# First product of the first four groups made token slot by token slot, and three smaller moves in a fused attention and feed-forward kernel

## The chip, the cores and the metric

The kernel runs on one core of one Trainium2 chip. The metric is the device time of one execution in microseconds (us), and the median of several executions is quoted. The kernel before took 298.68 us when it was first measured (three runs, 298.0 to 299.06). With each experiment it was run again on the same chip, and an experiment is compared with those runs only. All outputs of all kernels told here were correct.

An execution counts as slow when it lies more than 1.5% above the fastest of the same kernel.

## The reference

There are two parts in a row. Linear attention over 8 batches of 8 heads, 576 tokens, 64 features:

```python
q_p = phi(q, cos_w, sin_w); k_p = phi(k, cos_w, sin_w)   # relu, then cos and sin weights: 128 features
kv  = einsum('bhsf,bhsd->bhfd', k_p, v);  z = sum(k_p, axis=2)
num = einsum('bhsf,bhfd->bhsd', q_p, kv)
den = einsum('bhsf,bhf->bhs', q_p, z)[..., None] + 1e-06
x   = (num / den) with heads side by side: 4608 tokens x 512
```

and then a feed-forward layer on these 4608 tokens:

```python
h = x @ w_in                                 # 512 -> 2048
g = h * (1 / (1 + exp(-1.702 * h)))
out = g @ w_out                              # 2048 -> 512
```

## The kernel before

The tokens go in nine blocks of 512. In each block TensorE (PE) makes 16 groups of the first product (L278, "group 0" to "group 15", each of 128 hidden features), then the second product. Between these, pieces of the attention of the next batch are slipped in by a schedule `at(step, ...)`: q' and k' on DVE, the transposes of q' by DMA from the SP queue (`turn_q`), kv and z (`unit_kv`), and numerators (`unit_num`, 128 tokens, a "slot", at a time). The first batch has nothing to hide behind: its attention is the prologue.

```python
# order of the loads of the prologue, all from GpSimd's queue
load_main(0, "k", 0, 4)
load_main(0, "v", 0, 4)
load_main(0, "k", 4, 8)
load_main(0, "v", 4, 6)
load_main(0, "v", 6, 8)
...
# prologue, first product: three groups, 512 tokens wide, by quarters of the contraction as x comes
first = [mm_tile() for _ in range(3)]
for fc in range(3):
    mm1_first(fc, (0, 1), 0, TB)
    if fc == 1:
        turn_x0(0, 0, 4, 2, 3)
for fc in range(3):
    mm1_first(fc, (2,), 0, TB)
turn_x0(1, 0, 4, 3, 4)
for fc in range(3):
    mm1_first(fc, (3,), 0, TB, last=True)
    gelu(first[fc], fc)
...
def turn_q_at(b, c):                       # batch 1: q' turned by PE, copied out of PSUM by DVE
    t = at_tile()[:, 0].bitcast(BF16)...
    for h in range(H):
        nc.tensor.transpose(t[:, h], qn_slot(b, c)[:, h, :], ident[...])
    nc.vector.tensor_copy(q_slot(b, c)[:, :, 0:rows(c)], t)
...
# block i prepares batch b = i + 1
at(10, unit_num, 1, 4)                     # i == 1: the last 64 tokens of batch 1
at(22 + c // 2, turn_q_at, b, c)           # i == 0
at(k0 + c, turn_q, b, c)                   # i > 0: transposes by DMA
at(k1 - 1, prep_v, b, c)                   # v copied chunk by chunk
at(1, load_all, b + 1)                     # i > 0: the loads of the batch after
```

PSUM has two kinds of tile: four `mm` of one bank, two `at` of two banks. Matmuls on zeros (`warmup`) keep PE busy in the prologue.

## Time and profile before

| what | value | view |
|---|---|---|
| median of four runs of the first two rounds | 298.48 us | times |
| span of the profiled run | 296.7 us | page |
| PE busy | 97% of the span | page |
| first product at full size without a hole (group 4) | 23.43 us (the prediction and the expectations write 23.44) | PE timeline: 22.57 + 4 x 0.216 |
| group 4 to the first product after kv of batch 1 | 22.90 us | PE timeline: 46.33 - 23.43 |
| start of block 1 to slot 3's numerator of batch 2 | 24.48 us | PE timeline: 79.42 - 54.94 |

The lines of the profile that carry the argument are in the prediction below. Two of the page give the granted clock of TensorE, in tenths of full speed for each of 40 slices of the span (9 is 90% or more):

```profile
span 296.7 us, 5049 instructions
PEclk9999999999999999999999999999999999999999
```

(The clock record of this trace has it rise at 6.26 us and fall once, at 296.40. In it warm-up matmuls of 512 columns follow each other at 0.427 us before the rise and at 0.216 after it.)

### The profile page before, as it was taken

The numbers are of one execution on the slowest core, as the hardware profiler recorded it, in microseconds if no ns is written. First come the engines' busy times: TensorE is split into PE (matmuls) and PEld (weight loads), VectorE is DVE, ScalarE is ACT, GpSimd is POOL, SyncE is SP. The second block draws the span as 40 slices with busy tenths as digits, with TensorE's granted clock in tenths as the row PEclk, the third lists the DMA queues.
The fourth block names the chain that finished last, engine by engine and source line by source line (L and its number), as shares of the span: only waits on it lengthen the run. The fifth ranks groups of instructions, "written<-read, shape, count | busy, mean of one in ns | idle before, by whom it ended". The sixth has DMA issues, their size and how long they took to land.

```text
span 296.7 us, 5049 instructions
## 1 busy us (share of the span) xinstructions
PE 286.7 (97%) x1943; PEld 144.2 (49%) x1943; DVE 109.2 (37%) x363; ACT 121.4 (41%) x210; POOL 93.9 (32%) x117
## 2 busy tenths in 40 slices
PE   8779999999999999999999999999999999999994
PEld 3554456545444554455445544554455444444443
DVE  5850585772490158015811482148214200000000
ACT  5757401663126412651165116511651166127411
POOL 8443220620268025801690159004401200120021
PEclk9999999999999999999999999999999999999999
DMA  7999999699979967999799779975903610011033
GB/s 183 190 204 200 203 198 191 177 132 158 218 143 179 182 112 117 205 163 131 138 181 177 117 142 181 181 120 127 185 0 60 125 39 3 35 71 35 2 70 71
DMA packets 87303, 39.65 MB, mean 134 GB/s; under 512 B 57136, under 2 KB 85040, under 8 KB 87280
## 3 DMA queue, kind: packets, MB, share of 16 engines
q0 software_dynamic: 40848, 27.01, 59.7%
q1 hardware_dynamic: 46272, 12.20, 24.7%
q8 instruction: 15, 0.25, 0.3%
q10 hardware_dynamic: 160, 0.13, 0.2%
q14 instruction: 8, 0.07, 0.1%
HBM read 36.70 MB, written 9.44 MB: 155 GB/s over the span
## 4 chain that ended last, share of the span: by engine, by line
PE 89%; DMA 4%; ACT 3%; DVE 2%; issue 0%; DVEq 0%
PE mm L278 40%; PE mm L318 37%; DMA qT<-qn 4%; PE at L241 3%; PE at L262 3%; PE at L75 2%; PE mm L342 1%; ACT qT L362 1%; ACT kp L205 1%; DVE xb L270 1%; PE mm L409 1%; PE mm L371 1%; ACT xT L405 1%; PE at L222 0%; DVE qT L223 0%
## 5 line engine op out<-in xcount | busy, mean ns | idle before, releaser
L318 PE MATMUL mm<-w_out_sb,g 128*128 128x512 bf16 x560 | 128.7, 379 | 0.0
L278 PE MATMUL mm<-xT,w_in_sb 128*128 128x512 bf16 (+1 forms) x568 | 124.5, 378 | 0.0
L330 POOL DMA_DIRECT2D out_dram<-ysb x54 | 50.6, 941 | 174.3 <-ACT ysb L328 172.9
L283 ACT ACTIVATE g<-mm 128x512 bf16<-128x512 f32 x144 | 85.6, 597 | 47.3 <-PE mm L278 46.7
L278 PEld LDWEIGHTS <-w_in_sb 128*128 128x128 bf16 x568 | 54.7, 98 | 64.6
L318 PEld LDWEIGHTS <-g 128*128 128x128 bf16 x560 | 52.1, 97 | 57.0
L328 ACT COPY ysb<-mm 128x512 f32<-128x512 f32 x34 | 19.9, 585 | 98.2 <-PE mm L318 98.2
L245 DVE CAST kvs<-at 128x260 bf16<-128x260 f32 x14 | 5.4, 426 | 54.2 <-PE at L241 54.2
L270 DVE TENSOR_TENSOR xb<-at,inv 128x512 bf16<-128x512 f32 (+1 forms) x36 | 24.8, 690 | 1.2
L268 DVE TENSOR_SCALAR den<-at 128x8 f32<-128x8 f32 (+1 forms) x36 | 5.9, 164 | 46.5 <-PE at L262 46.5
L347 DVE COPY ysb<-mm 128x256 f32<-128x256 f32 x1 | 0.4, 426 | 59.4 <-PE mm L342 59.4
L207 DVE TENSOR_SCALAR qn<-q,cosw 128x512 bf16<-128x512 bf16 (+1 forms) x36 | 12.7, 357 | 13.6 <-DMA q<-in_q_dram 13.6
L262 PEld LDWEIGHTS <-qT 128*128 128x128 bf16 x272 | 12.9, 98 | 8.8 <-DMA qT<-qn 0.8
L262 PE MATMUL at<-kvs,qT 128*128 128x65 bf16 x272 | 14.3, 194 | 0.6 <-DMA qT<-qn 0.3
L207 DVE TENSOR_SCALAR qn<-q,sinw 128x512 bf16<-128x512 bf16 (+1 forms) x34 | 13.0, 381 | 0.0
L241 PEld LDWEIGHTS <-kp 128*128 128x128 bf16 (+1 forms) x288 | 10.1, 97 | 3.5 <-DVE vt L210 0.8
L241 PE MATMUL at<-vt,kp 128*128 128x65 bf16 (+1 forms) x288 | 11.3, 193 | 0.6 <-DVE vt L210 0.5
L86 POOL DMA_DIRECT2D v<-in_v_dram x10 | 8.5, 851 | 4.9 <-DMA v<-in_v_dram 2.5
L86 POOL DMA_DIRECT2D k<-in_k_dram x9 | 7.8, 864 | 2.7 <-DMA q<-in_q_dram 1.9
L230 ACT COPY xT<-at 128x512 bf16<-128x512 bf16 x4 | 2.4, 590 | 15.0 <-PE at L228 15.0
L75 PE MATMUL at<-warm 128*128 128x512 bf16 x19 | 7.2, 536 | 1.2 <-DVE eps L151 1.2
L207 DVE TENSOR_SCALAR kp<-k,cosw 128x512 bf16<-128x512 bf16 x24 | 8.4, 350 | 0.0
(75 smaller groups left out, 135.2 us busy)
## 6 DMA issues: line engine op xcount, KB each, us to landing
out_dram<-ysb POOLq DMA_DIRECT2D x38, 128.0 KB, 2.9
out_dram<-ysb POOLq DMA_DIRECT2D x16, 256.0 KB, 2.8
q<-in_q_dram POOLq DMA_DIRECT2D x7, 512.0 KB, 9.2
k<-in_k_dram POOLq DMA_DIRECT2D x6, 512.0 KB, 11.2
v<-in_v_dram POOLq DMA_DIRECT2D x6, 512.0 KB, 12.8
w_out_sb<-in_moe_w_out_dram POOLq DMA_DIRECT2D x4, 512.0 KB, 18.4
w_in_sb<-in_moe_w_in_dram POOLq DMA_DIRECT2D x3, 512.0 KB, 11.7
q<-in_q_dram SPq DMA_DIRECT2D x2, 512.0 KB, 4.6
```

What stands on the lines that cost most here:

```text
L75: nc.tensor.matmul(wps[:, 0], warm[:, 0:128], warm, start=True, stop=True)
L86: on.dma_start(out=state[b][n][:np_, t * D * h0:t * D * h1].rearrange("p (h e) -> p h e", h=h1 - h0), in_=SRC[n][b, h0:h1, 0:np_ * t, :].r ...
L207: nc.vector.tensor_scalar(oc, i, 0.0, wc, op0=MAX, op1=MUL)
L241: nc.tensor.matmul(kv[:, ds(h % 4 * (D + 1), D + 1)], kp[:r, c, h, :], vt[:r, c, h, 0:D + 1], start=(c == 0), stop=(c == last))
L262: nc.tensor.matmul(nm[:, h // 4, ds(h % 4 * (D + 1), D + 1)], q_slot(b, c)[:, h, :], state[b]["kvs"][:, h // 4, h % 4, 0:D + 1], start=Tru ...
L268: nc.vector.tensor_scalar(den[:r], nm4[:, :, :, D], 1e-6, None, op0=ADD)
L270: nc.vector.tensor_tensor(state[b]["xb"][:r, c].rearrange("p (n h) d -> p n h d", n=2), nm4[:, :, :, 0:D], inv[:r].unsqueeze(3).to_broadca ...
L278: nc.tensor.matmul(hps[:, c0:c1], w_in_sb[:, kc, ds(fc * 128, 128)], xT[:, kc, ds(i * TB + c0, c1 - c0)], start=(kc == 0), stop=(kc == KC ...
L283: nc.scalar.activation(g, hps, AF.Gelu_apprx_sigmoid)
L318: nc.tensor.matmul(yps, gT[fc][:, ds(t * 128, 128)], w_out_sb[:, fc, :], start=(fc == 0), stop=(fc == FC - 1))
L328: nc.scalar.copy(ysb, cur[t])
L330: nc.gpsimd.dma_start(out=out[row:row + (n - 1) * step + 1:step, :], in_=ysb[p0:p0 + n, :])
```

## The change

The change has three parts. In part A the prologue makes four groups of the first product instead of three, slot by slot as x comes (128, 128 and 256 tokens), turns x in the unused half of the bank that held the numerators, and loads k's upper half ahead of v's lower one. (It also has ACT copy all four pieces of the turned q', of which DVE copied one before, and loads the third group of w_in ahead of q's tail.) In part B the turned q' of batch 1 is copied out of PSUM by ACT instead of DVE, and its v by one DVE copy instead of six. In part C the numerator of batch 1's tail moves from step 10 to step 14 of block 1.

```diff
 # part A
+    load_main(0, "k", 4, 8)
     load_main(0, "v", 0, 4)
-    load_main(0, "k", 4, 8)
 ...
-    warmup(13)
+    warmup(12)
 ...
-    kv0(0, 4)
 ... (k' upper, numerators, turns and three groups of 512 columns)
+    kv_lo, kv_hi = mm_tile(), mm_tile()
+    kv0(kv_lo, 0, 4)
+    kv0(kv_hi, 4, 6)
+    na0 = num0(0, 0)
+    kv0(kv_hi, 6, 8)
+    product0(na0, den0(na0), 0, 0)
+    nb0 = num0(1, 0)
+    turn_x0(na0, 0, 0)
+    product0(nb0, den0(nb0, VE, (0, 1)), 1, 0, (0, 1))
+    product0(nb0, den0(nb0, VE, (1, 2)), 1, 0, (1, 2))
+    turn_x0(nb0, 1, 0, (0, 1))
+    first = [mm_tile() for _ in range(4)]
 ...
+    for fc in (0, 1):
+        mm1_first(fc, K4, 0, 128)
+    turn_x0(nb0, 1, 0, (1, 2))
 ... (128 to 256, then 256 to 512 in two halves of the contraction)
 # part B
-        nc.vector.tensor_copy(q_slot(b, c)[:, :, 0:rows(c)], t)
+        copy(q_slot(b, c)[:, :, 0:rows(c)], t)            # called with AC.copy
+    def prep_v_wide(b):
+        nc.vector.tensor_copy(vt[:96, :, :, 0:D], state[b]["v"][:96, 0:48 * D].rearrange(...))
 # part C
-                at(10, unit_num, 1, 4)
-                at(10, turn_x, 1, 4)
+                at(14, unit_num, 1, 4)
+                at(14, turn_x, 1, 4)
```

More of the change, by code (lines that the diff above doesn't have):

```diff
@@ L133 @@
     load_w_in(1)
+    load_w_in(2)
     load_tail(0, "q")
-    load_w_in(2)
     load_w_in(3)
@@ L207, in prep @@
                 nc.vector.tensor_scalar(oc, i, 0.0, wc, op0=MAX, op1=MUL)
+    def prep_v_wide(b):
+        nc.vector.tensor_copy(vt[:96, :, :, 0:D], state[b]["v"][:96, 0:48 * D].rearrange("p (h c d) -> p c h d", c=6, d=D))
     def prep_v(b, c, h0=0, h1=H):
@@ L217, in turn_q, with turn_q_at @@
                                     in_=qn_slot(b, c).rearrange("p h e -> p (h e)"))
-    def turn_q_at(b, c):
+    def turn_q_at(b, c, copy):
         t = at_tile()[:, 0].bitcast(BF16).rearrange("p (h t) -> p h t", h=H)[:, :, 0:rows(c)]
@@ L362, in turn_q0, with kv0 @@
         copy(qT[:, 4 * n:4 * n + 4, ds(256 * p, 256)].rearrange("p h (s t) -> p h s t", s=2), t)
-    def kv0(h0, h1):
-        kv = mm_tile()
+    def kv0(kv, h0, h1):
         v3 = s0["v"][:96].rearrange("p (j d) -> p j d", d=D)
@@ L370, in kv0 @@
                 j = h * 6 + c
-                nc.tensor.matmul(kv[:, ts(h - h0, 128)].rearrange("p (j d) -> p j d", j=2), kp[:96, c, h, :],
+                nc.tensor.matmul(kv[:, ts(h % 4, 128)].rearrange("p (j d) -> p j d", j=2), kp[:96, c, h, :],
                                  v3[:, j:49:48 - j, :], start=(c == 0), stop=(c == 5))
         nc.scalar.copy(s0["kvs"][:, h0 // 4, h0 % 4:h0 % 4 + h1 - h0, 0:D + 1],
-                       kv[:, 0:128 * (h1 - h0)].rearrange("p (h e) -> p h e", e=128)[:, :, 0:D + 1])
@@ L376, in num0 @@
-    def num0(c0, c1, h0, h1):
-        nm = at_tile().rearrange("p b e -> p (b e)").rearrange("p (s e) -> p s e", s=c1 - c0)
-        for s in range(c0, c1):
-            for h in range(h0, h1):
-                nc.tensor.matmul(nm[:, s - c0, ds((h - h0) * (D + 1), D + 1)], qT[:, h, ts(s, 128)],
-                                 s0["kvs"][:, h // 4, h % 4, 0:D + 1], start=True, stop=True)
-        return nm[:, :, 0:(h1 - h0) * (D + 1)].rearrange("p s (h e) -> p s h e", e=D + 1)
-    def den0(nm4, on=nc.vector):
-        den = two.tile([128, 8], F32, name="den").rearrange("p (s h) -> p s h", s=nm4.shape[1])
+                       kv.rearrange("p (h e) -> p h e", e=128)[:, h0 % 4:h0 % 4 + h1 - h0, 0:D + 1])
@@ new lines, in num0, with nm4, den0 @@
+    def num0(n, p):
+        nm = at_tile()
+        for s in range(2):
+            for h in range(4):
+                nc.tensor.matmul(nm[:, s, ds(h * (D + 1), D + 1)], qT[:, 4 * n + h, ts(2 * p + s, 128)],
+                                 s0["kvs"][:, n, h, 0:D + 1], start=True, stop=True)
+        return nm
+    def nm4(nm, s0_, s1):
+        return nm[:, s0_:s1, 0:4 * (D + 1)].rearrange("p s (h e) -> p s h e", e=D + 1)
+    def den0(nm, on=nc.vector, s=(0, 2)):
+        den = two.tile([128, 8], F32, name="den").rearrange("p (s h) -> p s h", s=2)[:, 0:s[1] - s[0]]
@@ L387, in den0, with product0 @@
         if on is nc.scalar:
-            nc.scalar.activation(den, nm4[:, :, :, D], AF.Identity, bias=eps)
+            nc.scalar.activation(den, nm4(nm, *s)[:, :, :, D], AF.Identity, bias=eps)
         else:
-            nc.vector.tensor_scalar(den, nm4[:, :, :, D], 1e-6, None, op0=ADD)
+            nc.vector.tensor_scalar(den, nm4(nm, *s)[:, :, :, D], 1e-6, None, op0=ADD)
         return den
-    def product0(nm4, den, c0, c1, h0, h1):
-        inv = two.tile([128, 8], F32, name="inv").rearrange("p (s h) -> p s h", s=c1 - c0)
+    def product0(nm, den, n, p, s=(0, 2)):
+        k = s[1] - s[0]
+        inv = two.tile([128, 8], F32, name="inv").rearrange("p (s h) -> p s h", s=2)[:, 0:k]
@@ L395, in product0 @@
         nc.vector.reciprocal(inv, den)
-        nc.vector.tensor_tensor(s0["xb"][:, c0:c1, h0:h1, :], nm4[:, :, :, 0:D],
-                                inv.unsqueeze(3).to_broadcast([128, c1 - c0, h1 - h0, D]), op=MUL)
-    def turn_x0(m, c0, c1, j0, j1):
-        w = tp[:, ts(m, 512)].rearrange("p (j s t) -> p j s t", j=j1 - j0, t=128)
-        for c in range(c0, c1):
-            for j in range(j0, j1):
-                nc.tensor.transpose(w[:, j - j0, c - c0], s0["xb"][:, c, 2 * j:2 * j + 2, :]
+        nc.vector.tensor_tensor(s0["xb"][:, 2 * p + s[0]:2 * p + s[1], 4 * n:4 * n + 4, :], nm4(nm, *s)[:, :, :, 0:D],
+                                inv.unsqueeze(3).to_broadcast([128, k, 4, D]), op=MUL)
@@ L404, in turn_x0 @@
+    def turn_x0(nm, n, p, s=(0, 2)):
+        w = nm.rearrange("p b e -> p (b e)").bitcast(BF16).rearrange("p (b e) -> p b e", b=2)[:, :, 768:1024]
+        for c in range(*s):
+            for j in range(2):
+                nc.tensor.transpose(w[:, c, ts(j, 128)], s0["xb"][:, 2 * p + c, 4 * n + 2 * j:4 * n + 2 * j + 2, :]
                                     .rearrange("p h d -> p (h d)"), ident)
-        nc.scalar.copy(xT[:, j0:j1, c0 * 128:c1 * 128], w.rearrange("p j s t -> p j (s t)"))
-    def mm1_first(fc, kcs, c0, c1, last=False):
+        nc.scalar.copy(xT[:, 2 * n:2 * n + 2, (2 * p + s[0]) * 128:(2 * p + s[1]) * 128]
+                       .rearrange("p j (s t) -> p s j t", t=128),
+                       w[:, s[0]:s[1]].rearrange("p s (j t) -> p s j t", j=2))
@@ L408, in mm1_first @@
+    def mm1_first(fc, kcs, c0, c1):
         for kc in kcs:
             nc.tensor.matmul(first[fc][:, c0:c1], w_in_sb[:, kc, ts(fc, 128)], xT[:, kc, c0:c1],
-                             start=(kc == 0), stop=(last and kc == KC - 1))
+                             start=(kc == 0), stop=(kc == KC - 1))
     AC, VE = nc.scalar, nc.vector
     kvs_new(0)
-    warmup(13)
+    warmup(12)
     def prep_q0(n, p, on=(VE, VE)):
@@ L418, in prep_q0 @@
         prep(0, "q", 2 * p + 1, 4 * n, 4 * n + 4, on=on)
+    prep_q0(0, 0, (VE, AC))
+    prep_q0(0, 1, (VE, AC))
     for n, p in ((0, 0), (0, 1), (1, 0), (1, 1)):
-        prep_q0(n, p, on=(VE, VE if n else AC))
-        turn_q0(n, p, VE.tensor_copy if (n, p) == (1, 1) else AC.copy)
-        warmup(2)
-        if (n, p) == (1, 0):
-            prep_q0(1, 1)
-            for c in range(6):
-                prep(0, "k", c, 0, 4, on=(VE, AC if c > 2 else VE))
-            turn_q0(1, 1, VE.tensor_copy)
-            break
@@ L430 @@
-    kv0(0, 4)
-    for c in range(2, 6):
-        prep(0, "k", c, 4, 8, on=(VE, AC))
-    for c in range(2):
-        prep(0, "k", c, 4, 8)
-    na = num0(0, 2, 0, 4)
-    nb = num0(2, 4, 0, 4)
-    da, db = den0(na), den0(nb, AC)
-    product0(na, da, 0, 2, 0, 4)
-    product0(nb, db, 2, 4, 0, 4)
-    tp = mm_tile().bitcast(BF16)
-    kv0(4, 6)
-    turn_x0(0, 0, 2, 0, 2)
-    kv0(6, 8)
-    na = num0(0, 4, 4, 6)
-    turn_x0(1, 2, 4, 0, 2)
-    product0(na, den0(na), 0, 4, 4, 6)
-    na = num0(0, 4, 6, 8)
@@ L448 @@
-    product0(na, den0(na), 0, 4, 6, 8)
-    first = [mm_tile() for _ in range(3)]
-    for fc in range(3):
-        mm1_first(fc, (0, 1), 0, TB)
-        if fc == 1:
-            turn_x0(0, 0, 4, 2, 3)
-    for fc in range(3):
-        mm1_first(fc, (2,), 0, TB)
-    turn_x0(1, 0, 4, 3, 4)
-    for fc in range(3):
-        mm1_first(fc, (3,), 0, TB, last=True)
+        if n:
+            prep_q0(n, p)
+        turn_q0(n, p, AC.copy)
+        if (n, p) != (1, 1):
+            warmup(2)
+    for n in range(2):
+        for c in range(6):
+            prep(0, "k", c, 4 * n, 4 * n + 4, on=(VE, AC if c > 2 else VE))
@@ new lines @@
+    kv_lo, kv_hi = mm_tile(), mm_tile()
[10 more added lines that the diff above has]
+    first = [mm_tile() for _ in range(4)]
+    na1 = num0(0, 1)
+    product0(na1, den0(na1, AC), 0, 1)
+    K4 = (0, 1, 2, 3)
+    for fc in (0, 1):
+        mm1_first(fc, K4, 0, 128)
@@ L459 @@
+    turn_x0(nb0, 1, 0, (1, 2))
+    for fc in (2, 3):
+        mm1_first(fc, K4, 0, 128)
+    for fc in (0, 1):
+        mm1_first(fc, K4, 128, 256)
+    nb1 = num0(1, 1)
+    product0(nb1, den0(nb1), 1, 1)
+    turn_x0(na1, 0, 1)
+    for fc in (2, 3):
+        mm1_first(fc, K4, 128, 256)
+    for fc in range(4):
+        mm1_first(fc, (0, 1), 256, 512)
+    turn_x0(nb1, 1, 1)
+    for fc in range(4):
+        mm1_first(fc, (2, 3), 256, 512)
         gelu(first[fc], fc)
@@ L488 @@
                 if i == 0:
-                    at(22 + c // 2, turn_q_at, b, c)
+                    at(22 + c // 2, turn_q_at, b, c, AC.copy)
                 else:
@@ L493 @@
                 at(20 if i == 0 else k1 - 4 + c // 2, prep, b, "k", c)
-                at(k1 - 1, prep_v, b, c)
+                if b >= 2:
+                    at(k1 - 1, prep_v, b, c)
+            if b == 1:
+                at(k1 - 1, prep_v_wide, b)
             at(k1, unit_kv, b)
@@ L505 @@
             if n < FC:
-                if i > 0 or n > 2:
+                if i > 0 or n > 3:
                     mm1(i, n)
```

## The prediction

> **What bounds the kernel now.** I read the page's busy table, then the chain of waits, then the table of stretches, then each engine's timeline of the first 80 us.
>
> ```profile
> PE 286.7 (97%) x1943; PEld 144.2 (49%) x1943; DVE 109.2 (37%) x363; ACT 121.4 (41%) x210; POOL 93.9 (32%) x117
> 87.00:290.00 203.00, 203.00 (x1289) 98.93 (x1287) 57.51 (x195) 83.27 (x140) 61.58 (x68) 1.00 0.72 114
> ```
> The first line (engine, busy us) says TensorE is the bound. The second (stretch, length, then busy us of PE, PEld, DVE, ACT, POOL) says that from 87 us on PE has no hole. So the change can only win in the holes before that, and only by bringing forward the moment at which PE leaves its last one. The PE timeline shows them, by what ended each:
>
> ```profile
> 11.20 0.63 PE L371 MATMUL mm<-v,kp 96*128 96x128 bf16 x4 [0.26 <-DMA v<-in_v_dram]
> 14.09 0.67 PE L381 MATMUL at<-kvs,qT 128*128 128x65 bf16 x16 [0.47 <-ACT kvs L373]
> 18.30 1.02 PE L409 MATMUL mm<-xT,w_in_sb 128*128 128x512 bf16 x4 [0.38 <-ACT xT L405]
> 21.93 0.81 PE L409 MATMUL mm<-xT,w_in_sb 128*128 128x512 bf16 x3 [0.67 <-ACT xT L405]
> 22.57 9.66 PE L278 MATMUL mm<-xT,w_in_sb 128*128 128x512 bf16 x44
> 44.04 2.46 PE L241 MATMUL at<-vt,kp 96*128 96x65 bf16 x48 [0.27 <-DVE vt L210]
> 66.78 2.05 PE L241 MATMUL at<-vt,kp 128*128 128x65 bf16 x40 [0.19 <-DVE vt L210]
> 79.42 0.43 PE L262 MATMUL at<-kvs,qT 128*128 128x65 bf16 x8 [0.33 <-DMA qT<-qn]
> ```
> Four places: the prologue (to 22.57, where full-size products begin), kv of batch 1 at 44, kv of batch 2 at 66.8, and the numerator of slot 3 of batch 2 at 79.4, which waits for a DMA transpose. The bracket is only the hole before the group: 48 kv matmuls take 1.46 us when fed (the chain: 43 in 1.46), but at 44 they take 2.46 from start to end, because the copies of v arrive one by one.
>
> The inputs of the prologue land in a row. DVE's timeline gives 9.87 for k's lower half and 12.71 for its upper half ([0.40 <-DMA k<-in_k_dram]); PE's gives 11.20 for v's lower half. From issue times and times to landing: v heads 4-5 issued 3.84 + 9.5 = 13.3, heads 6-7 at 14.06, w_in group 0 at 5.10 + 10.3 = 15.4 and 5.8 + 10.8 = 16.65.
>
> [...] the warm-up matmuls follow each other at 0.42 us until 6.28 and at 0.216 after. [...] Six copies of 512 took 1.29 us, that is 0.20 each[...]. [...]
>
> ```profile
> 57.76 15.65 SPq L216 DMA_TRANSPOSE qT<-qn  x5
> 84.44 7.58 SPq L216 DMA_TRANSPOSE qT<-qn  x5
> ```
> (SP queue: start, us.) The same five transposes take twice as long to issue while batch 3's loads run.
>
> **Part A, the prologue.** Removed: one warm-up matmul, three-group first products of 512 columns, extra mm banks for turned x. Added: four groups, as 16 products each of 128, 128 and 256 columns. PE work is the same per column: 128-column transposes follow each other at 0.056 us and 512-column products at 0.216, so 32 x 0.056 + 16 x 0.11 = 3.55 against 16 x 0.216 = 3.46. Moved: k's upper half ahead of v's lower, so k lands at 11.2 and **v's lower half at 12.7**.
>
> DVE's q work is unchanged (last at 9.27). ACT's two sines of q come first now; its four qT copies run 6.93, 7.84, 8.92, 9.97 (1.01 each, 0.91 when back to back). So k's six ACT sines run 10.9 to 13.4 (0.40 apart), DVE's 18 from 9.87 to 13.5 (0.196 apart). That is better than before, where upper k was done at 15.6. But kv of heads 0-3 cannot start before v at 12.73:
>
> - kv 0-3: 24 x 0.056, ends 14.24 (before 13.63). ACT kvs copy 14.28-14.65. kv 4-5 ends 14.91, copied by 15.22.
> - numerators na0 14.75-15.17. kv 6-7 15.27 (bank) to 16.11, copied by 16.42. Numerators nb0 16.47-16.95.
> - DVE: na0 (0.17 + 0.20 + 0.69, with gaps 1.14) to 16.35; nb0 slot 0, 256 columns at an estimated 0.42, to 17.66; slot 1 to 18.43; na1 to 19.52.
> - PE turns na0 at 16.75, ACT copies it 17.16-17.74; turns nb0 slot 0 at 17.71, copied by 18.39 (estimated 0.37 for 256 columns).
> - first products of slot 0: 18.44, two groups, then turn, two groups to 19.45; slot 1's copy lands 19.57, its products 19.62 on, with nb1 and the turn of na1 between them, to 21.0.
> - na1's copy ends 21.34: products of slots 2 and 3, lower half of the contraction, 21.39-22.27; turn nb1, ACT copy 22.70-23.28; upper half 23.33-24.21.
> - all four mm banks are now in use, so group 4 waits for gelu of group 0: 23.75 + 0.60, start at 24.40.
>
> Before, group 4 starts at 22.57 + 4 x 0.216 = 23.44. **A costs +0.96**: about 0.6 from v landing later, the rest from five ACT round trips (copy 0.37-0.59 and two hand-overs) that PE has too little to cover, and the gelu wait; what the earlier upper half wins is spent there.
>
> **Part B, batch 1's q' and v.** Removed from DVE: four q' copies (two pairs at 1.29) and six v copies in a row behind them (1.29). Added: four ACT copies (1.01, ACT is idle from 34.9 to 49.9) and one v copy of 3072[...], right behind k' at 40.1, done by 41.1. In the times of before: turns of slots 0, 1 at 40.09, ACT copies 40.74-41.75 and to 42.66; slot 2 turned at 41.85; slot 3 waits for its bank until 42.71 (new wait, 0.4); out products to 44.02; kv 44.02-45.48 without stops. Before, the next product starts at 46.33: **B saves 0.85**.
>
> **Part C, numerator of batch 1's tail from step 10 to 14.** DVE no longer waits 1.43 us for PE in front of k' and v of batch 2. kv of batch 2 then runs in its 1.21 and PE is at 67.4 where it was at 68.67 - 0.25: 1.03 less. But the way leads to 79.42. PE would come there at 78.06 instead of 79.09; slot 3's transpose lands at about 79.4 because SP's issues (one each 4 us) are held by the loads, not by PE. **C moves the hole and saves about 0**; I grant 0.3 for a transpose that lands a little earlier.
>
> The loads of batch 3 and the q transposes both start at the end of block 0 (56.75 and 57.76), so A and B shift all of this together. Sum: 298.68 + 0.96 - 0.85 - 0.3 = 298.5; I take 298.4.
>
> **Rivals.**
> 1. *All three parts pay.* If A's waits are shorter (the copies overlapped better than my serial hand-overs), A is 0, and C keeps its 1.03: 298.68 - 0.85 - 1.03 = 296.8. For it: each idle hole named in the timeline is addressed. Against: v at 12.7 is a landing, and the 0.33 wait on the transpose existed already.
> 2. *The transposes' hole grows.* As central, with C nothing: 298.8. For it: SP's 15.65 us.
> 3. *The clock falls.* PE is idle from 9.9 to 12.73 in the new order, 2.8 us[...]. If it falls to half clock then, about 3 us of dense PE work doubles in part: +1.5 to 2, 300 or a bit more. For it: two warm-ups per turn no longer bridge to kv. [...]
> 4. *False sharing.* If the products of slot 0 wait for the copy of slot 1 (same xT rows, other columns), A costs another 0.5. Nothing in before shows it: there a product never followed a copy of other columns of its rows.
>
> **Range and chances.** The timed runs of before spread over 1.06 us by themselves. A is uncertain by 0.7, B by 0.2, C by 0.5 on the side of a gain, the clock by 1.5 with one chance in seven. That gives 296.8 to 299.9. A move of 2% is 6.0 us, more than three times all holes that the change addresses in B and C together, and A cannot win more than about 3 (the holes from 11 to 22.6 and the gap to v): faster 0.02, slower 0.02.
>
> **What would show it.** The first kv matmul at 12.7 with v's DMA as its releaser; first 128-column product near 18.4; full-size products from about 24.4, the first of them behind a gelu; L241's 48 matmuls in about 1.6 us near 44, with ACT copying q'; no hole at kv of batch 2; and a hole of about 1.3 us in place of 0.33 before slot 3's numerator at 79.4. I am wrong if full-size products begin before 23.4 (A gains), if the hole at 79 stays near 0.3 (C pays), or if matmuls after 12.7 follow at 0.11 us instead of 0.056 (clock).

## The result, and the profile after

The changed kernel took 301.36 us in the median (300.75, 302.53, 301.96 and 300.68), the kernel before 298.48 us (298.0 to 299.06) in the same rounds. A ratio here is the mean time of one kernel's fast runs over that of the other's of the same rounds, so it isn't quite the ratio of the medians. It is 1.01, with a 95% interval of 1.0058 to 1.0142. The change costs about 1%, and all four runs lie outside the predicted range of 296.8 to 299.9. All outputs are right.

The page of the changed kernel, with the lines that answer to those of before:

```profile
span 298.8 us, 5123 instructions
PE 287.7 (96%) x1974; PEld 148.5 (50%) x1974; DVE 106.1 (36%) x357; ACT 126.0 (42%) x215; POOL 95.0 (32%) x117
PEclk9879999999999999999999999999999999999999
```

The second and third slice of the clock (7.5 to 22.4 us) are no longer at full speed. The mean granted clock of the four runs was 0.989, 0.975, 0.989 and 0.983, against 0.999 in the profiled run of before. The profiled run of the changed kernel (0.989) shows two stretches of 3.41 us at half clock. So one of them is worth about 0.0057, which is 3.41 / 2 over 298.8, and by this estimate 0.983 and 0.975 stand for three and about four. The estimate is rough, since the clock also falls at the end of a span, after PE's last matmul (in before at 296.40, after one that ended at 292.82): c_only below has 0.997 from that alone.

The PE timeline of the changed kernel (start us, us, engine, line, operation, output<-inputs, count, and in brackets the hole before it and what ended that):

```profile
9.11 0.78 PE L364 MATMUL mm<-ident,qn 128*128 128x128 bf16 x8
12.47 3.58 PE L373 MATMUL mm<-v,kp 96*128 96x128 bf16 x36 [2.58 <-DMA v<-in_v_dram]
...
19.68 0.27 PE L409 MATMUL at<-ident,xb 128*128 128x128 bf16 x2 [1.44 <-DVE xb L401]
...
20.08 1.14 PE L417 MATMUL mm<-xT,w_in_sb 128*128 128x128 bf16 x8
...
26.38 1.03 PE L417 MATMUL mm<-xT,w_in_sb 128*128 128x256 bf16 x8 [0.67 <-ACT xT L411]
27.45 8.79 PE L281 MATMUL mm<-xT,w_in_sb 128*128 128x512 bf16 x40
...
46.78 0.61 PE L225 MATMUL at<-ident,qn 128*128 128x128 bf16 x8 [0.31 <-ACT qT L226]
48.09 1.61 PE L244 MATMUL at<-vt,kp 96*128 96x65 bf16 x48
...
69.38 1.37 PE L244 MATMUL at<-vt,kp 128*128 128x65 bf16 x40
...
81.42 0.43 PE L265 MATMUL at<-kvs,qT 128*128 128x65 bf16 x8 [0.16 <-DMA qT<-qn]
```

The reader is to see four things. The 36 kv matmuls of the prologue take 3.58 us. From 13.17 on they start 0.107 us apart, where at full clock they follow at 0.056. Group 4 (the first line of L281) starts at 27.45, 4.0 us later than the 23.43 of before. The kv of batch 1 now takes 1.61 instead of 2.46, and that of batch 2 takes 1.37 instead of 2.05 with its hole gone. The hole before slot 3's numerator of batch 2 is 0.16.

The same first stretch by windows of 3.41 us. In the trace's record the clock rises at 6.34, 16.58 and 23.41 and falls at 13.17 and 20.00, so these moments are one or two times 3.41 us apart, and the windows are cut at them and halfway between those that are two apart (columns: stretch, length, busy us and count of PE, PEld, DVE, ACT, POOL, then clock, DMA share and GB/s):

```profile
9.76:13.17 3.41, 0.82 (x14) 0.69 (x12) 3.41 (x18) 3.37 (x8) 1.96 (x3) 1.00 1.27 195
13.17:16.58 3.41, 3.41 (x39) 3.38 (x36) 0.32 (x2) 0.81 (x3) 2.62 (x4) 0.50 1.24 205
16.58:20.00 3.42, 1.68 (x33) 1.51 (x32) 2.46 (x9) 0.86 (x3) 0.78 (x1) 1.00 1.34 201
20.00:23.41 3.41, 3.41 (x42) 3.32 (x39) 0.90 (x2) 0.95 (x3) 1.31 (x2) 0.50 1.30 205
```

A window in which PE did little is followed by one at half clock, twice. In the first pair PE was busy for 0.82 of 3.41 us. In the second it was busy for 1.68 of 3.42 us, and still the clock fell.

Stage by stage, in the two profiled runs (a minus is earlier or shorter):

| stage | before | after | difference | forecast |
|---|---|---|---|---|
| start to group 4 | 23.43 | 27.45 | +4.02 | +0.96 |
| group 4 to the first product after kv of batch 1 | 22.90 | 22.09 | -0.81 | -0.85 |
| start of block 1 to slot 3's numerator of batch 2 | 24.48 | 23.27 | -1.2 | -0.3 |
| sum, with what lies between | | | +2.06 | -0.2 |

After that point PE has no hole in either kernel: the first product of L281 in block 2 starts at 88.91 instead of 86.85, and the span ends 2.1 later.

### The profile page after: what moved, and what is told of

Read it like the earlier page. It is cut to its first block, busy times and chain, and to the rows that moved or that the text cites.

```text
span 298.8 us, 5123 instructions
## 1 busy us (share of the span) xinstructions
PE 287.7 (96%) x1974; PEld 148.5 (50%) x1974; DVE 106.1 (36%) x357; ACT 126.0 (42%) x215; POOL 95.0 (32%) x117
## 4 chain that ended last, share of the span: by engine, by line
PE 88%; DMA 7%; DVE 2%; ACT 1%; POOL 1%; issue 1%; POOLq 0%; DVEq 0%; ACTq 0%
PE mm L281 40%; PE mm L321 37%; DMA qT<-qn 4%; DMA v<-in_v_dram 3%; PE at L244 3%; PE at L265 3%; PE mm L417 2%; PE mm L373 1%; PE mm L345 1%; DVE xb L273 1%; ACT qT L226 1%; PE at L382 1%; POOL k L86 0%; ACT xT L411 0%; PE at L225 0%
## 5 line engine op out<-in xcount | busy, mean ns | idle before, releaser
L281 PE MATMUL mm<-xT,w_in_sb 128*128 128x512 bf16 (+1 forms) x564 | 123.6, 377 | 0.0
L281 PEld LDWEIGHTS <-w_in_sb 128*128 128x128 bf16 x564 | 54.3, 98 | 64.1 <-issue 0.2
L86 POOL DMA_DIRECT2D v<-in_v_dram x10 | 9.3, 942 | 5.7 <-DMA w_in_sb<-in_moe_w_in_dram 2.8
L244 PE MATMUL at<-vt,kp 128*128 128x65 bf16 (+1 forms) x288 | 9.8, 193 | 0.0
L207 DVE TENSOR_SCALAR kp<-k,sinw 128x512 bf16<-128x512 bf16 x24 | 8.1, 339 | 0.0
```

Source lines behind the costliest of these rows:

```text
L86: on.dma_start(out=state[b][n][:np_, t * D * h0:t * D * h1].rearrange("p (h e) -> p h e", h=h1 - h0), in_=SRC[n][b, h0:h1, 0:np_ * t, :].r ...
L207: nc.vector.tensor_scalar(oc, i, 0.0, wc, op0=MAX, op1=MUL)
L244: nc.tensor.matmul(kv[:, ds(h % 4 * (D + 1), D + 1)], kp[:r, c, h, :], vt[:r, c, h, 0:D + 1], start=(c == 0), stop=(c == last))
L281: nc.tensor.matmul(hps[:, c0:c1], w_in_sb[:, kc, ds(fc * 128, 128)], xT[:, kc, ds(i * TB + c0, c1 - c0)], start=(kc == 0), stop=(kc == KC ...
```

## The experiments

The theory was that the two falls of the clock cost the prologue its 3 us, and that they come when PE does too little within a window of 3.41 us, the length of each of the two half-clock stretches. One rival was that part A is slow by itself, through its ACT round trips and false waits, and the clock only goes with that. Another was that it is one unbroken idle stretch of PE that makes the clock fall. For the last two stages, the rivals were whether B and C pay alone, and what holds the transpose before slot 3's numerator.

To compare windows across kernels I use one measure. The share of a window is the number of columns that PE's matmuls streamed in it, at 2,400 per us (1,200 at half clock), over 3.41 us. The rates are my rounding of the traces: 512 columns take 0.427 us at half clock in before (1,199 per us) and 128 take 0.107 in the changed kernel (1,196), and 2,400 is twice 1,200. Measured at full clock, 512 columns take 0.216 us (2,370 per us) and 128 take 0.056. A window without a hole at full clock so comes to 0.99 (23.33 to 26.74 in before) and not to 1. The share is lower than the busy time of the profile, which contains pipeline time: 0.17 and 0.37 for the two windows of the changed kernel ahead of its falls. Windows that end after PE's last matmul are left out until the end of the account; each of the 14 profiles has one more fall there, after a window of 0.26 or less (in before 292.98 to 296.40, without a matmul).

### warm1: twelve warm-up matmuls while v is on its way

```diff
-        if (n, p) != (1, 1):
-            warmup(2)
+        warmup(2 if (n, p) != (1, 1) else 12)
```

> The changed kernel with twelve warm-up matmuls (12 x 0.216 = 2.6 us at full clock) put into the empty stretch of TensorE between the last turn of q and the first kv matmul, which waits for v. Clock theory: the first stretch of half clock (13.17 to 16.58 in the profile of after) goes; 36 kv matmuls take about 2.1 us instead of 3.58; full-size products begin 1.4 us earlier, near 26.0, or near 24.6 if the second stretch (19.99 to 23.41) goes as well. Rival, waits: the 3.06 us by which the prologue missed the forecast are hand-overs and false dependencies; then filling a stretch in which TensorE waits for v anyway moves the beginning by less than 0.3.

Measured: 299.63 us in the median against 298.55, ratio 1.0007 (0.9977 to 1.0037). The profiled run fell in the slow state (302.76), so its total isn't used, but its prologue shows no fall. (Nor do those of warm2 and warm1_own, which have the same twelve matmuls and whose profiles are of fast runs.) PE timeline:

```profile
9.69 2.75 PE L75 MATMUL at<-warm 128*128 128x512 bf16 x11
12.47 2.27 PE L373 MATMUL mm<-v,kp 96*128 96x128 bf16 x36
...
24.74 5.56 PE L281 MATMUL mm<-xT,w_in_sb 128*128 128x512 bf16 x24
...
81.87 0.53 PE L265 MATMUL at<-kvs,qT 128*128 128x65 bf16 x8 [2.49 <-DMA qT<-qn]
```

The kv matmuls start at the same 12.47 as in the changed kernel, take 2.27 instead of 3.58, and group 4 starts 2.71 earlier, at 24.74. Both falls are gone with work that computes nothing. Two of the six runs, those at clock 1.0, took 297.82 and 297.45. The three other fast ones had a clock of 0.994, which is one fall by the estimate above, and took 299.61 to 299.74. The profiled run shows where such a fall can come from: a hole of 2.49 us before slot 3's numerator of batch 2 (after one of 0.65 a slot earlier), and half clock from 82.03 to 85.45. So a hole there can take back what the prologue gains. That the repair made it longer isn't shown: warm2 below begins group 4 0.3 us earlier still, and has only a small hole.

### warm2: five more while the second product of x is made

```diff
 # on top of warm1
     turn_x0(na0, 0, 0)
+    idle = mm_tile()
+    for _ in range(5):
+        nc.tensor.matmul(idle, warm[:, 0:128], warm, start=True, stop=True)
```

> As the first, with five more warm-up matmuls (1.08 us) into a free bank in the hole of 1.44 us before the turn of slot 0 of the second numerator. Clock theory: no stretch of half clock remains after 6.3 us, 16 products of 128 columns take 0.056 us each, full-size products begin at 24.4 to 24.8 (2.7 to 3.0 earlier than in after). Waits theory: no gain, or a loss by the added matmuls. If in addition the transposes of batch 2 are held by a backlog of loads that does not move with the prologue, the hole before the numerator of slot 3 of batch 2 grows from 0.16 to about 1, and the total gains only about 2.

Measured: 300.22 us against 298.55, ratio 1.0063 (1.0023 to 1.0102), with runs from 297.59 to 301.95. The profiled run is the best of them (297.59, span 295.6): full-size products from 24.46, no fall, only a small hole before slot 3's numerator. So the prologue is settled by warm1, and the five more gain nothing that the spread would let one see. Two of the longer runs (301.34 and 301.76) have clocks of 0.993 and 0.994, but 301.95 came at 1.0 and has no profile. What it spent its time on is open.

### warm1h and warm1q: six and three warm-up matmuls instead of twelve

```diff
-        warmup(2 if (n, p) != (1, 1) else 12)
+        warmup(2 if (n, p) != (1, 1) else 6)     # warm1h; 3 in warm1q
```

> The changed kernel with six warm-up matmuls (1.3 us) in the empty stretch instead of twelve. In the runs so far every window of 3.41 us with a busy share of 0.37 or less was followed by half clock and none with 0.50 or more. The window of the stretch, 0.17 to 0.29 busy without them, comes to 0.55 to 0.67: no fall there if the rule is a share of a window. If the rule were an unbroken idle stretch of some length, 1.3 us left open would be as safe.

> As above with three (0.65 us): the share comes to 0.36 to 0.48, about where the limit should lie; the empty stretch left is near 2 us. A fall in some executions and not in others, by where the window lies, would bear out the share; no fall at all would put the limit below 0.36.

Measured: 297.95 us against 298.66 for six (ratio 0.9964, 0.9929 to 0.9999), and 299.16 for three (ratio 0.999, 0.9941 to 1.0039, one slow run of 302.83 left out). They were run on another chip. In the profiles of both the first fall is gone and the second one stays: half clock at 19.09 to 22.51 with six, at 17.95 to 21.37 with three. The profile of warm1q is that of the slow run, which fell once more at 82.80, after a hole of 2.52 us before slot 3's numerator. Its windows ahead of and in the fall of the prologue, in the columns used above:

```profile
14.54:17.95 3.41, 1.57 (x27) 1.38 (x26) 2.50 (x9) 0.93 (x3) 1.75 (x3) 1.00 1.24 208
17.95:21.37 3.42, 3.42 (x40) 3.42 (x39) 0.89 (x2) 1.01 (x3) 0.78 (x1) 0.50 1.39 199
```

The first of these windows has a share of 0.34, and its longest unbroken hole is 1.44 us. The profile of warm1h, a fast run, shows the same: the window ahead of its fall (15.68 to 19.09) has a share of 0.31 and the same longest hole, 1.44. That speaks against the rival of one unbroken idle stretch. Two of the three fast runs of warm1q stayed at clock 1.0 and one at 0.989, so the same program falls in some executions and not in others. In the profiles the first rise to full clock came at another moment in each execution (4.30 to 6.95 us). Windows counted from that moment begin elsewhere each time, which puts the same holes into other windows.

### vfirst: v's lower half loaded ahead of k's upper half again

```diff
+    load_main(0, "v", 0, 4)
     load_main(0, "k", 4, 8)
-    load_main(0, "v", 0, 4)
```

> The changed kernel with v's lower half loaded ahead of k's upper half again, as before; nothing else. Clock theory: TensorE's empty stretch shrinks from 2.58 to about 1.3 us, the window of 3.4 us in which it lies is over half busy, the first stretch of half clock goes, and full-size products begin 1.5 to 3 us earlier than 27.46. Waits theory: kv of heads 0-3 is done about 1 us earlier, but kv of heads 6-7 is not, since upper k comes later; gain under 0.5.

Measured: 300.66 us against 298.55, ratio 1.0061 (1.0026 to 1.0096), one slow run of 303.44 left out. The first kv matmul starts at 11.20 after a hole of 1.31, half as long as the 2.58 of the changed kernel. The clock fell all the same: half clock from 12.40 to 22.64, three windows, and full-size products only from 27.33. The window ahead, 8.99 to 12.40, had a share of 0.29. My expectation that the fall would go was wrong, and for a reason that helps: I had taken the window to be over half busy, since its hole is short, and had not counted the columns in it.

### warm1_own: the first slot turned in a bank of its own

```diff
 # on top of warm1; turn_x0 gets a parameter that names where the turned x goes
-    turn_x0(nb0, 1, 0, (0, 1))
+    turn_x0(nb0, 1, 0, (0, 1), into=mm_tile())
```

> The changed kernel with the twelve warm-up matmuls, and slot 0 of the second numerator turned into a bank of its own instead of the numerators' tile. If the hole of 1.44 us before that turn is a wait for the product of slot 1, which reads the same tile: it shrinks to about 0.7 and full-size products begin 0.6 to 0.8 earlier than 24.74, near 24.0, still not earlier than the 23.44 of before. Rival: the wait is for the product of slot 0 itself or for TensorE's own order, and nothing moves.

In the changed kernel, the two slots of nb0 lie in one `at` tile. DVE made their products one after the other:

```profile
18.46 0.42 DVE L401 TENSOR_TENSOR xb<-at,inv 128x256 bf16<-128x256 f32 x1
19.20 0.42 DVE L401 TENSOR_TENSOR xb<-at,inv 128x256 bf16<-128x256 f32 x1
```

The turn of slot 0 could have started at 18.88, but it started at 19.68 (the line with the hole of 1.44 above), just after the second product, which ended at 19.62. The turned x goes into the tile that the second product was still reading, so it waited for that too.

Measured: full-size products from 23.91 instead of 24.74, 0.83 earlier (expected 24.0). It was run on another chip. The time was 299.51 us against 298.57, ratio 1.0005 (0.9966 to 1.0044). What the prologue gained was lost in batch 2, as this stretch and its numerator show:

```profile
76.10:79.51 3.41, 2.16 (x16) 0.95 (x16) 1.06 (x3) 0.59 (x1) 0.00 (x0) 1.00 1.55 128
79.51:82.93 3.42, 1.46 (x14) 0.86 (x15) 0.92 (x3) 0.00 (x0) 1.04 (x2) 1.00 1.17 210
...
81.47 0.43 PE L265 MATMUL at<-kvs,qT 128*128 128x65 bf16 x8 [2.68 <-DMA qT<-qn]
```

The first two lines are of the windows view, the third of the PE timeline. The hole of 2.68 us is longer than the 2.58 of the changed kernel's prologue, and yet the clock did not fall. The hole lies across two windows, whose shares are 0.56 and 0.41. This is the other half of the test against an unbroken idle stretch.

### b_only, c_only and bc: parts B and C in the kernel before

The three take the diff's parts B, C and both, and leave the prologue as it was.

> The kernel before with part B alone. From the runs so far: block 0 ends 0.81 us earlier; the hole before the numerator of slot 3 of batch 2 is 0.33 as before, since loads and transposes start from the end of block 0. Total 0.6 to 0.9 faster than before. Rival: the transposes are tied to loads that do not move, the hole grows to about 1.1, total unchanged.

> The kernel before with part C alone. As predicted: TensorE reaches the numerator of slot 3 of batch 2 about 1.0 us earlier and waits there about 1.3 us in place of 0.33, total within 0.3 of before. Rival, C pays: total 0.8 to 1.1 faster.

> The kernel before with parts B and C alone (q' of batch 1 by ACT, v copied at once, numerator of the tail at step 14), its prologue untouched. As predicted: B saves 0.81 to 0.85 up to the end of block 0; C moves its hole to 79.4: hole there 1 us or more in place of 0.33, total 0.5 to 0.9 faster than before. Rival, C pays: the hole stays at 0.2 to 0.4 and the total is 1.8 to 2.0 faster.

| kernel | median, us | before, us | ratio | 95% interval |
|---|---|---|---|---|
| b_only | 297.75 | 298.57 | 0.9969 | 0.9953 to 0.9985 |
| c_only | 298.56 | 298.57 | 0.9992 | 0.9974 to 1.001 |
| bc | 297.29 | 298.55 | 0.9962 | 0.994 to 0.9984 |

The PE timelines of c_only and of bc, one line of each, at slot 3's numerator of batch 2:

```profile
78.74 0.43 PE L262 MATMUL at<-kvs,qT 128*128 128x65 bf16 x8 [1.58 <-DMA qT<-qn]
```

```profile
77.82 0.43 PE L265 MATMUL at<-kvs,qT 128*128 128x65 bf16 x8 [1.17 <-DMA qT<-qn]
```

B alone gains 0.8 us. C alone shows no gain: the hole at kv of batch 2 goes (40 matmuls in 1.37), and the hole of 0.33 before slot 3's numerator becomes 1.58. This is what the prediction said. The changed kernel without its prologue is 0.4% faster than before in these runs, but bc_late below, the same kernel in effect, gave 1.0003 on another chip, so that gain isn't certain.

### bc_late: batch 3's loads registered seven steps later

```diff
 # on top of bc
-                at(1, load_all, b + 1)
+                at(1 if i > 1 else 8, load_all, b + 1)
```

> B and C on the kernel before, with batch 3's loads issued at step 8 of block 1 instead of step 1, behind the transposes of batch 2. If the loads hold the transposes: SP issues all five in 6 to 8 us instead of 15, no hole near 78 (1.17 in the run with B and C), total 1.0 to 1.3 faster than with B and C, near 296.1. If something else paces the transposes (SP itself, their writes), the hole stays near 1.2 and nothing is gained.

This failed as an experiment. GpSimd had nothing else to wait for and issued the first of the loads at 55.92, as it would have anyway, so the kernel is bc over again. It measured 298.46 us against 298.57 (ratio 1.0003, 0.9963 to 1.0042), with runs from 297.44 to 301.74 and holes of 0.47 and 1.86 in its profile. What it teaches is the spread that this hole brings, and that a later place in the program didn't hold the loads back.

### bc_gate: batch 3's loads behind a dependency

```diff
 # on top of bc
+def load_gated(b, i):
+    if i == 1:
+        nc.gpsimd.tensor_copy(gate, kp[:, 2, 0, 0:2])   # waits for k' of batch 2
+    load_all(b)
...
-                at(1, load_all, b + 1)
+                at(9 if i == 1 else 1, load_gated, b + 1, i)
```

> B and C on the kernel before, with batch 3's loads really held back this time: GpSimd first copies two elements of k' of batch 2 (written by VectorE near 62), so that its loads go out about 6 us later. In the run meant to do this by program order alone they went out at 55.9 as ever, so it was a repeat of B and C. If the loads hold the transposes: SP issues the five transposes of batch 2 in 6 to 9 us instead of 15, no hole before slot 3's numerator, total 1.0 to 1.3 faster than B and C and with less spread: near 296.3. If SP or the transposes themselves are the pace: issues stay near 4 us each, hole 1 to 2.

Measured: **295.47 us** against 298.66, ratio **0.9885** (0.9857 to 0.9912). The five runs lie between 295.43 and 295.50, where those of before lie between 298.34 and 300.83. Three lines, of the timelines of the SP queue, GpSimd and PE:

```profile
56.08 6.74 SPq L226 DMA_TRANSPOSE qT<-qn  x5
...
59.70 0.24 POOL L107 COPY gate<-kp 128x2 bf16<-128x2 bf16 x1 [4.62 <-DVE kp L214]
...
76.20 0.42 PE L272 MATMUL at<-kvs,qT 128*128 128x65 bf16 x8
```

GpSimd waits 4.62 us for k', the loads start at 59.93 instead of 55.35 in bc, the five transposes are issued in 6.74 us instead of 15.68, and the numerator of slot 3 has no hole before it. So the loads did hold the transposes. (own_gate and warm1_own show it once more: 7.85 us with the gate and 16.94 without.) The gain beyond bc, which ran on another chip, is 1.6 us of span (293.5 against 295.1), of which 1.17 is the hole and 0.29 an earlier group 4 (22.55 against 22.84).

One caution: this profiled run had an early first rise of the clock, at 4.42 us, and group 4 started at 22.55, while the first profile of before had 6.26 and 23.43. The old prologue follows that moment: 22.54 in c_only with a rise at 4.35, 23.39 in b_only with one at 6.19. The moment of the rise in the unprofiled runs isn't recorded, so I can't say how much of the 3.2 us belongs to it. From the two profiles I estimate 0.9 at most, though the mean of before over 11 runs should hold early rises too. The five runs of bc_gate lie within 0.07 us, so either all had about the same rise or it moves the end by less than it moves group 4; the record doesn't say which.

### own_gate: the changed kernel with all three repairs

This is the changed kernel with twelve warm-ups, the bank of warm1_own and the dependency of bc_gate.

> The changed kernel with its clock held (twelve warm-up matmuls), slot 0 turned into a bank of its own and batch 3's loads held back. If the account of the loss is complete, it stands 0.5 us behind the run with B and C and held loads, which is the prologue's remaining deficit (23.9 against 23.44): near 296.8, and faster than before. If something else of the change costs time, it stays at 298 or above.

Measured: 296.60 us against 298.66, ratio 0.9921 (0.9899 to 0.9944), runs from 296.33 to 296.85, no fall in the profile, products of full size from 23.60. It is faster than before, but 1.13 behind bc_gate on the same chip (0.5 was expected), and no run of the one overlaps with a run of the other. Both have B, C and the gate, so the rest is the prologue: 23.60 against 22.55 in these profiles, which is 1.05. By these times the new prologue loses to the old one even with its clock and its false wait repaired. The caution above holds here too: the rise came at 6.66 in this profile, and the old prologue with a late rise, 23.43, would be only 0.17 ahead. The new prologue didn't follow the rise: it has 23.60 here and 23.91 in warm1_own, where the rise came at 4.42.

## Why the prediction was wrong, and where it was right

**The step that failed is the clock.** The sum for part A took PE to run at full clock through the wait for v. The prediction named a fall of the clock as its rival 3 and gave it "one chance in seven". That was an estimate of mine: it went by the length of one hole, 2.8 us, and no trace of before showed after what the clock falls while the kernel still has work. In the runs, over all 14 profiles and 1,163 windows at full clock, the clock fell after every window with a share of 0.365 or less, which were seven, and after none with 0.41 or more. Four of the seven are in profiles of fast runs: 0.17 and 0.365 in the changed kernel, 0.29 in vfirst and 0.31 in warm1h. Three are in the two profiles of slow runs, among them the 0.34 of warm1q. The pair warm1h or warm1q (longest hole 1.44, fell) and warm1_own (hole 2.68, did not) separates the share of a window from an unbroken idle stretch. The prediction also looked for one fall. There were two in the profiled run, because the hole of 1.44 before 19.68, about half of it a false wait (below), made a second thin window. With that wait gone as well, in warm1_own, the window there had 0.46 and no fall came. The prologue of before already had windows of 0.63, 0.58 and 0.53 (6.26 to 16.50), the last not far above the 0.41 that was the lowest without a fall, so there was little to give away.

**Its size.** The rival was put at +1.5 to 2. Measured, group 4 goes from 27.45 to 24.74 with twelve warm-ups and to 24.46 with five more, where v came 0.19 earlier, so the half clock cost 2.7 to 3.0. That covers nearly all of the 3.05 between forecast and measurement (24.40 and 27.45), and is why the rival's "300 or a bit more" was too low for the 301.36 measured.

**Part A without the clock** was forecast at +0.96 and measured at +1.0 to +1.3 (24.46 and 24.74 against 23.43, in profiles whose clock rose late in all three, at 6.95, 6.94 and 6.26 us). As forecast, the first full-size product was released by a gelu. v landed somewhat before the forecast: the first kv matmul started at 12.47 instead of 12.73. The wait that the prediction marks "(bank)" was there: ACT's copy of heads 4-5 ended at 16.36 in the changed kernel, and the kv matmuls of heads 6-7 started at 16.42. A part of the delay that the prediction didn't have is a false wait, of the kind of its rival 4 but at another place: not the product behind a copy, but the turn of slot 0 behind the product of slot 1. A bank of its own gave 0.83 back. So it is in part luck that the forecast of 24.40 came within 0.34 of the 24.74 of warm1: the wait that it lacked was made up in part by v's earlier landing and by steps that went faster than forecast.

**Part B** was forecast at 0.85 and measured at 0.81 between the two profiles. b_only gave 0.3% of 298.6, the same 0.8 or 0.9. The wide v copy, to which the prediction gives 1.0 (40.1 to 41.1, an estimate of mine that no copy in before shows), took 0.94, and the wait for the bank of slot 3, forecast at 0.4, was 0.31.

**Part C** was right in its mechanism: a hole that moves from kv of batch 2 to the transpose. c_only has it at 1.58 and bc at 1.17, where the prediction said about 1.3. But in the changed kernel's own profile the mark set for it failed: the hole was 0.16 and the stage gained 1.2. By the prediction's own test this would mean that C pays. The times of the DMA offer another reading. The GpSimd timelines of before and then of the changed kernel give the moment at which the first of batch 3's loads was issued:

```profile
56.75 0.92 POOL L86 DMA_DIRECT2D q<-in_q_dram  x1
```

```profile
59.96 0.92 POOL L86 DMA_DIRECT2D q<-in_q_dram  x1
```

By the DMA view, slot 3's transpose landed at 79.38 and at 81.37, so 22.6 us after that moment in before and 21.4 us after it in the changed kernel. That is the 1.2 by which the stage got shorter. PE was ready 1.0 us earlier within its block, as forecast (at 81.26, which is 23.11 after the start of block 1, against 79.09, which is 24.15 after it), and the hole stayed small because the landing came earlier as well. The same time is 22.8 in c_only, 22.4 in bc, 19.7 in warm1h and 25.0 in warm1_own. So a difference of 1.2 lies within what this time does from profile to profile, and the gain of the stage can't be put down to C. The forecast of 0.3 was mis-sized because it took the landing as nearly fixed. What makes the landing come early or late, as long as loads and transposes run together, stays open.

**The step behind C**, that SP's transposes are held by the loads of batch 3 and not by PE, was right, and bc_gate shows it by taking the loads away: 6.74 us instead of 15.68 for five.

**The sum.** The forecast of the stages was +0.96, -0.85 and -0.3. The profiles gave +4.02, -0.81 and -1.2. The -1.2 lies within the spread told above. The timed runs are 2.9 above those of before in the median, more than the 2.1 between the profiles. The lower clock can account for the run of 302.53 (0.975), but not for that of 301.96, whose 0.989 is that of the profiled run (300.75). A slip of the prediction changed nothing: 22.57 + 4 x 0.216 is 23.43 and not 23.44.

**What stays open.** No window at full clock with work after it had a share between 0.365 and 0.41, so the runs don't show what comes after such a one. With the windows at the end of the spans counted, one of 0.372 in warm2 (290.26 to 293.67) was not followed by a fall, while that of 0.365 in the changed kernel was. Nor do these shares settle when the clock rises again: it rose after all half-clock windows of 0.92 or more but one, of 0.95 in vfirst (12.40 to 15.81), where it also stayed at half after 0.66 and then rose after 0.79. If each matmul's columns are weighted with the input rows that the timeline gives for it (96*128 for the prologue's kv, so 96 of 128), the window of 0.95 has 0.73. That was tried after the fact and is one window, so it would need a test of its own. Why the hole before slot 3's numerator is 0.2 in one profile and 2.7 in another isn't settled either, beyond that it goes when the loads do.

## What to carry to other kernels

Where PE waits in pieces, read the granted clock and count PE's work in windows cut at the moments at which it changes, and don't look for the longest hole. In before and the changed kernel these moments lay 3.41 us apart or a multiple of it. The clock was at half here after each of the seven windows with a share of 0.365 or less, and it stayed at full across a hole of 2.68 us (warm1_own, windows of 0.56 and 0.41). Twelve matmuls on zeros into a free bank took both falls of the prologue away (group 4 at 24.74 instead of 27.45) without delaying the work behind them (kv at 12.47 in both). A piece that was to go ahead by itself needed a tile of its own here, or it waited for the last reader of its neighbour (0.83 us). The loads were held back by a dependency (to 59.93) and not by their place in the program (55.92), and holding one set of them back for 4.6 us, behind transposes that are needed sooner, gave 1.6 us of span here.
